# Lightning attention followed by a cosine-gated feed-forward: the loads of q, k and v for two sequences joined into one transfer from the fifth pair on

## The chip, the cores and the metric

The kernel runs on one core of a Trainium2 chip. The metric is the device time of one execution in microseconds. Seven executions of the kernel before gave a median of 203.84 us, from 203.79 to 204.97.

## What is computed

Four sequences of 768 positions, eight heads of 64 channels. The attention is linear with a decay per head: within a block the scores are masked by powers of `lam`, and between blocks a 64 by 64 state per head is carried along. The heads of each position are put together to a row of 512, and a feed-forward layer with the gate h * cos(h) follows.

```python
for b in range(nb):
    intra = einsum('bhic,bhjc->bhij', qb, kb) * Dmask
    intra = einsum('bhij,bhjd->bhid', intra, vb)
    inter = einsum('bhid,bhde->bhie', qb * lam_pow, kv_state)
    out[:, :, sl] = intra + inter
    kv_state = lam_block * kv_state + einsum('bhsd,bhse->bhde', kb * rev_pow, vb)
x = attn_out.transpose(0, 2, 1, 3).reshape(B * S, H * D)      # 3072 x 512
h = x @ w_in                                                   # 3072 x 2048
out = (h * cos(h)) @ w_out                                     # 3072 x 512
```

Inputs and output are float32; the matrix products run in bf16.

## The kernel before

The 3072 positions are cut into 24 blocks of 128. Two blocks make a pair, and there are 12 pairs, counted here from 0 as in the code. Pairs 0 and 1 (`SPANS = 2`) are loaded and computed in a form of their own at the start. From pair 2 on, pair `pr` consists of block `2*pr` and block `2*pr+1`, which are the same 128 positions of two neighbouring sequences (`where`, line 167, gives sequence `b` and position chunk `c`). "The fifth pair" is pair 4, `n = 8` and up.

One pair goes through these steps:

- `add_load` (L289): SyncE starts six transfers, one each of q, k and v for both blocks: `q_f`, `k_f`, `v_f`, tiles of 128 positions by 8 heads by 64 floats, 256 KB each. In HBM 64 floats (256 B) lie together. Each of the three names has six buffers.
- `prepare` (L329): GpSimd turns them into bf16: `prep_q` (L343) scales q, `prep_k` (L347) casts k, both into the halves of one tile `qk`; `prep_v` (L351) scales v into `v_s`. Its order is q, q, k, k, v, v. Pair 2 alone uses VectorE and ScalarE for a part of it.
- From pair 3 on (`DMA_FROM = 6`) SyncE starts two transposing transfers from `qk` into `qkT` (L379), the first for q, the second for k. The first waits for both `prep_q`, the second for both `prep_k`.
- TensorE makes the scores from `qkT` (L421) and the state update from `qk` and `v_s` (L433), VectorE masks the scores (L426) and adds up the state (L439), TensorE makes the values (L484) and adds the part of the carried state (L516), and the result goes to `xT`.
- The feed-forward part takes tiles of two or four blocks (`TILES`): TensorE multiplies `xT` by `w_in` (L746, 16 groups of four matmuls for a tile), ScalarE takes the cosine (L752), VectorE multiplies (L758), TensorE multiplies by `w_out` (L792, 16 matmuls for a block), ScalarE moves the result to `o_sb` (L806), and SyncE stores it (L813, L815).

The order on every engine is fixed when the kernel is built. `Planner.order` (L70) plays all tasks through with the durations that the code gives them, always starting the task that can begin first, and the instructions are written out in the order of the starts. On TensorE a pair's scores are therefore put at the place at which the plan believes its `qkT` to be there. A load is planned as `dma("SP", LOAD_US, 0.85, ...)` (L302): 0.85 us on SyncE's queue, then 1.22 us on the transfer engines, then 1.0 us until it can be read. Each engine carries out its list strictly in order, so an instruction that waits holds up all behind it.

On SyncE's queue the order in the loop is, for one pair: two q loads, two k loads, two v loads, the two transposes, with one or two stores of finished blocks among them. The q load of pair `pr+1` is planned after the second transpose of pair `pr` (L388).

Of the kernel before, what the change touches and what calls it, by code (L numbers as in the profile page):

```python
# [10 lines left out]
F32 = mybir.dt.float32  # L11
# [12 lines left out]
LAG = 2  # L24
ATT = 0.95
LOAD_US = 1.22
ALONE = [3, 4, 5, 6]

APART = [3, 4, 5, 11]
# [113 lines left out]
def kernel(  # L143
# [10 lines left out]
    nc = tc.nc  # L154
    B, H, S, D = q.shape
    P = 128
# [10 lines left out]
    def where(n):  # L167

        if n < 2 * SPANS:
            return n // 2, n % 2  # L170
        g, c = divmod(n // 2, NB)
        return 2 * g + n % 2, c

    BUFS = {"ld": 6, "qk": 3, "v_s": 6, "qkT": 3, "s_m": 4, "cos": 3, "o_sb": 4}
    ctx.enter_context(tc.manual_schedule())
    consts = ctx.enter_context(tc.tile_pool(name="consts", bufs=1))
    loads = ctx.enter_context(tc.tile_pool(name="loads", bufs=BUFS["ld"]))
    toks = ctx.enter_context(tc.tile_pool(name="toks", bufs=4))
    work = ctx.enter_context(tc.tile_pool(name="work", bufs=2))
    psum = ctx.enter_context(tc.tile_pool(name="psum", bufs=1, space=bass.MemoryType.PSUM))  # L180
# [1 line left out]
    def bank(i, shape, dt, name):  # L182
        return psum.tile(shape, dt, tag=f"bank{i}", bufs=1, name=name)
# [54 lines left out]
    w_out_src = moe_w_out.rearrange("(ko ki) m -> ki ko m", ki=P)  # L238
    WCH = 4

    pl = Planner({**BUFS, "q_f": BUFS["ld"], "k_f": BUFS["ld"], "v_f": BUFS["ld"]})
    MM = lambda cols, n=1: n * (cols / 2400.0 + 0.0025)

    SW = 0.11
# [1 line left out]
    live = {}  # L246
# [4 lines left out]
    def prio_attn(n, part):  # L251
        i = next(i for i in range(len(TILES)) if n < first[i + 1])
        return begins[i - 1] + unit[i - 1] * (n - n % 2 - first[i] + 2 * part) / TILES[i]

    load_t, issue_t = {}, {}
    last_issue = {}

    def dma(queue, us, issue_us, emit, prio, deps=(), get=None, ordered=True, lat=1.9):
        t = pl.add(queue, issue_us, list(deps) + [last_issue.get(queue) if ordered else None], emit, prio, get=get)
        if ordered:  # L260
            last_issue[queue] = t
        d = pl.add("DMA", us, [t], None, prio, lat=lat)
        d.issue = t
        return t, d

    def start(queue, o, x, deps):
        i = queue.dma_start(out=o, in_=x)  # L267
        for d in deps:
            tc.add_manual_dep(i.ins, d.issue.ins.ins.name, mybir.DependencyInfo(
                mybir.DependencyClass.Sync, mybir.DependencyReason.DATA), reason="order of loads")  # L270
        return i
# [16 lines left out]

    def add_load(n, name, src, prio, deps=()):  # L289
        b, c = where(n)  # L290

        def emit(_):
            t = loads.tile([P, H, D], F32, tag=name, name=name)
            live[name, n] = t
            i = start(nc.sync, t, src[b, :, c * P:(c + 1) * P, :].transpose([1, 0, 2]), deps)
            if (name, n) == ("q_f", 2 * SPANS):

                tc.add_manual_dep(i.ins, pace[0].ins.ins.name, mybir.DependencyInfo(
                    mybir.DependencyClass.Sync, mybir.DependencyReason.DATA), reason="order of loads")
            return i  # L300

        issue_t[name, n], load_t[name, n] = dma("SP", LOAD_US, 0.85, emit, prio, deps, get=name,  # L302
                                                lat=1.9 if name == "v_f" and n < 2 * SPANS + 2 else 1.0)
        return load_t[name, n]

    w_t, pace = {}, []
# [22 lines left out]
    def prepare(pr):  # L329

        b, c = where(2 * pr)
        early = 2 * pr < TILES[0] + 2
        vec = {"DVE": nc.vector, "POOL": nc.gpsimd}
        us = {"DVE": 0.69, "POOL": 1.05}
        pa = lambda part: prio_attn(2 * pr, part)

        def new_qk():
            if ("qk", pr) not in live:
                live["qk", pr] = toks.tile([P, 2, H, 2, D], BF16, tag="qk", bufs=BUFS["qk"], name="qk")
            return live["qk", pr]  # L340

        def prep_q(_, s, e):
            vec[e].tensor_mul(new_qk()[:, 0, :, s], live.pop(("q_f", 2 * pr + s)),  # L343
                              q_scale[:, c, :].unsqueeze(2).to_broadcast([P, H, D]))

        def prep_k(_, s):
            (nc.scalar.copy if early else nc.gpsimd.tensor_copy)(new_qk()[:, 1, :, s], live.pop(("k_f", 2 * pr + s)))  # L347

        def prep_v(_, s, e):
            live["v_s", 2 * pr + s] = toks.tile([P, H, D], BF16, tag="v_s", bufs=BUFS["v_s"], name="v_s")  # L350
            vec[e].tensor_mul(live["v_s", 2 * pr + s], live.pop(("v_f", 2 * pr + s)),  # L351
                              v_scale[:, c, :].unsqueeze(2).to_broadcast([P, H, D]))

        a, k_ = [], []
        for s in range(2):
            n = 2 * pr + s
            eq = "DVE" if early and s == 0 else "POOL"
            ev = "DVE" if early and s == 1 else "POOL"
            a.append(pl.add(eq, us[eq], [load_t["q_f", n]] + a, partial(prep_q, s=s, e=eq), pa(-0.9), get=None if s else "qk"))
            k_.append(pl.add("ACT" if early else "POOL", 0.61, [load_t["k_f", n]] + ([] if early else [a[0]]), partial(prep_k, s=s), pa(-0.9)))  # L360
            d_t[n] = v_head[n] = pl.add(ev, us[ev], [load_t["v_f", n]], partial(prep_v, s=s, e=ev), pa(-0.85), get="v_s")
            for name, t in (("q_f", a[s]), ("k_f", k_[s]), ("v_f", d_t[n])):
                issue_t[name, n].frees = [t]

        def new_T():
            if ("qkT", pr) not in live:
                live["qkT", pr] = toks.tile([P, 2, H, P], BF16, tag="qkT", bufs=BUFS["qkT"], name="qkT")
            return live["qkT", pr]

        def transposes(t, i):  # L370
            live["t", pr, i] = bank(t.bank[0], [P, H, P], BF16, "ps_t")
            for h in range(H):
                nc.tensor.transpose(live["t", pr, i][:, h, :], live["qk", pr][:, i, h], ident)  # L373

        def transposes_out(_, i):
            nc.vector.tensor_copy(new_T()[:, i], live["t", pr, i])

        def transposes_dma(_, i):
            return nc.sync.dma_start_transpose(out=new_T()[:, i], in_=live["qk", pr][:, i].rearrange("t h s d -> t (h s d)"))  # L379

        for i, src in enumerate((a, k_)):
            get = None if i else "qkT"
            if 2 * pr >= DMA_FROM:
                head, T[pr, i] = dma("SP", 1.4, 1.3, partial(transposes_dma, i=i), 2 * pr + i - LAG + 1.5,
                                     src + ([qkT_head[pr]] if i else []), get=get, ordered=False)
                T[pr, i].lat = 1.2
                if i and 2 * pr + LAG < NBLK:
                    issue_t["q_f", 2 * pr + LAG].deps.append(head)  # L388
            else:
                t = pl.add("PE", MM(P, 8), src + ([T[pr, 0]] if i else []), partial(transposes, i=i), pa(-0.05 + 0.05 * i), banks=1)  # L390
                head = T[pr, i] = pl.add("DVE", 0.7, [t], partial(transposes_out, i=i), pa(0.0), get=get)
                t.bank_frees = [[head]]
            if i == 0:
                qkT_head[pr] = head
        qk_head[pr] = a[0]
# [76 lines left out]
    def add_stretch(pr, ahead=None):  # L472
# [70 lines left out]
        deps = [So[n0], So[n0 + 1], Uo[pr, 0], Uo.get((pr - 1, 1)) if c else None]  # L543
        more = pr + 1 < NBLK // 2 and pr + 1 not in ALONE
        apart = pr in APART
# [279 lines left out]
    names = ORDER.split()  # L825
    for pr in range(SPANS, NBLK // 2):
        for name in "qkv":
            names += [x for x in (f"{name}{2 * pr}", f"{name}{2 * pr + 1}") if x not in names]
    src = {"q": q, "k": k, "v": v}
    kept = []  # L830
    for at, name in enumerate(names):
        which, n = name[0], int(name[1:])
        soft = which in "io"
        deps = [kept[-3 if soft else -2]] if at and (names[at - 1][0] in "io") != soft else []
        if name == f"q{2 * SPANS}":
            deps = []
        if name == f"v{2 * SPANS}":
            deps = [load_t["k_f", 2 * SPANS]]
        if name == "o3":
            deps = [load_t["q_f", 2 * SPANS]]  # L840
# [10 lines left out]
    for pr in range(SPANS, NBLK // 2):  # L851
        prepare(pr)
    first_scores, first_update = add_scores(SPANS, prio_attn(2 * SPANS, 0.2))
    add_span_state(first_scores, prio_attn(2 * SPANS, 0.2))
    pr = SPANS
    for i in range(len(TILES)):
        while 2 * pr < first[i + 1]:
            if pr + 1 in ALONE:
                add_scores(pr + 1, prio_attn(2 * pr + 2, 0.2))
# [64 lines left out]
```

## Time and profile before

The profiled execution took 203.82 us on the device, of which the profile's span covers 202.1 us; 1.7 us lie around it.

| engine | busy us | share of the span | instructions |
|---|---|---|---|
| TensorE, matmuls | 196.9 | 97% | 2469 |
| TensorE, weight loads | 116.8 | 58% | 2469 |
| ScalarE | 120.6 | 60% | 241 |
| VectorE | 116.2 | 57% | 228 |
| GpSimd | 64.8 | 32% | 85 |

| transfers | bytes | share of 16 engines |
|---|---|---|
| started by SyncE and ScalarE (q1) | 28.78 MB | 64.3% |
| started by GpSimd (q0) | 4.72 MB | 16.2% |

Times in the profile count from the start of the span. Busy time is summed by engine; "idle before" is what an engine stood still ahead of an instruction and what ended that; PE is the matmul part of TensorE and PEld its weight loads; SPq is SyncE's queue, where the time of an instruction includes what it is held back by a full queue.

### The profile page before, as it was taken

Reading aid. Unit: us, or ns where it says so; the run is one execution under the profiler, and the core shown is the slowest. Engines: PE = TensorE matmul, PEld = TensorE weight load, DVE = VectorE, ACT = ScalarE, POOL = GpSimd, SP = SyncE. Lnnn points to the kernel's source line nnn. Section 1 sums busy time; section 2 is a strip of 40 time slices with the busy share of each in tenths; the row PEclk is TensorE's granted clock in tenths of the full one; section 3 lists DMA queues with packets and bytes.
Section 4 is the critical chain, followed back from the end, with each engine's and each line's share of the span. In section 5 each row is a group of like instructions: output and inputs, shape, how many; then the busy total and the mean of one; then the engine's idle time right before and its main releaser. Section 6 shows DMA issues by size and latency. Waiting matters only on the chain.

```text
span 202.1 us, 5941 instructions
## 1 busy us (share of the span) xinstructions
PE 196.9 (97%) x2469; PEld 116.8 (58%) x2469; DVE 116.2 (57%) x228; ACT 120.6 (60%) x241; POOL 64.8 (32%) x85
## 2 busy tenths in 40 slices
PE   6999999999999999999999999999999999999994
PEld 2467444557757857767658676755445444444443
DVE  2878773257955958758448575834579544444001
ACT  4978870238838868565639666654877554355120
POOL 5694002076134173645555072533530000000000
PEclk9999999999999999999999999999999999999999
DMA  4999999999989998999999797999950010111112
GB/s 118 324 192 203 203 205 215 175 219 245 212 208 178 241 223 197 248 181 258 202 256 246 175 233 96 269 124 264 243 139 3 3 52 0 52 55 52 52 52 104
DMA packets 96762, 33.94 MB, mean 168 GB/s; under 512 B 84320, under 2 KB 93792, under 8 KB 96736
## 3 DMA queue, kind: packets, MB, share of 16 engines
q1 hardware_dynamic: 89232, 28.78, 64.3%
q0 software_dynamic: 7360, 4.72, 16.2%
q8 instruction: 19, 0.31, 0.7%
q14 instruction: 7, 0.06, 0.1%
q10 hardware_dynamic: 144, 0.07, 0.1%
HBM read 27.27 MB, written 6.29 MB: 166 GB/s over the span
## 4 chain that ended last, share of the span: by engine, by line
PE 93%; DMA 3%; SPq 2%; POOL 1%; issue 0%; ACT 0%; POOLq 0%; ACTq 0%
PE ps_h L746 42%; PE ps_f L792 42%; DMA sp_f<-in_k_dram 3%; PE ps_s L421 2%; PE ps_o L484 2%; PE ps_o L516 2%; PE ps_kv L433 1%; SPq L267 1%; PE ps_o L650 1%; PE ps_kv L637 1%; POOL k_sp L605 1%; PE ps_x L484 0%; PE ps_t L373 0%; PE ps_t L613 0%; PE ps_s L624 0%; PE ps_o L656 0%
## 5 line engine op out<-in xcount | busy, mean ns | idle before, releaser
L758 DVE TENSOR_TENSOR g<-ps_h,cos 128x256 bf16<-128x256 f32 (+1 forms) x148 | 73.2, 503 | 43.1 <-ACT cos L752 42.1
L752 ACT ACTIVATE cos<-ps_h,halfpi 128x256 f32<-128x256 f32 (+1 forms) x148 | 75.7, 539 | 29.4 <-PE ps_h L746 28.6
L792 PE MATMUL ps_f<-w_out_sb,g 128*128 128x512 bf16 (+2 forms) x400 | 91.5, 371 | 0.0
L746 PE MATMUL ps_h<-xT,w_in_sb 128*128 128x256 bf16 (+1 forms) x592 | 91.3, 304 | 0.0
L746 PEld LDWEIGHTS <-w_in_sb 128*128 128x128 bf16 x592 | 57.1, 98 | 30.1 <-DVE xT L524 0.4
L792 PEld LDWEIGHTS <-g 128*128 128x128 bf16 x400 | 37.7, 98 | 37.3
L343 POOL TENSOR_TENSOR qk<-q_f,q_scale 128x512 bf16<-128x512 f32 x19 | 19.8, 1056 | 35.1 <-DMA q_f<-in_q_dram 31.9
L806 ACT COPY o_sb<-ps_f 128x512 f32<-128x512 f32 (+1 forms) x24 | 13.8, 573 | 24.7 <-PE ps_f L792 24.7
L351 POOL TENSOR_TENSOR v_s<-v_f,v_scale 128x512 bf16<-128x512 f32 x19 | 19.7, 1043 | 17.8 <-DMA v_f<-in_v_dram 12.7
L426 DVE TENSOR_TENSOR s_m<-ps_s,mask 128x512 bf16<-128x512 f32 x20 | 13.0, 685 | 4.2 <-PE ps_s L421 3.6
L347 POOL CAST qk<-k_f 128x512 bf16<-128x512 f32 x18 | 11.0, 614 | 10.4 <-DMA k_f<-in_k_dram 10.3
L524 ACT CAST xT<-ps_o 128x512 bf16<-128x512 f32 x11 | 6.0, 588 | 9.2 <-PE ps_o L516 5.8
L439 DVE TENSOR_TENSOR sum<-sum,ps_kv 128x512 f32<-128x512 f32 x15 | 10.2, 681 | 0.6
L444 ACT CAST S<-sum 128x512 bf16<-128x512 f32 x15 | 9.2, 617 | 0.9 <-DVE sum L439 0.8
L267 POOL DMA_DIRECT2D w_out_sb<-in_moe_w_out_dram x4 | 3.0, 776 | 15.9 <-DMA q_f<-in_q_dram 15.9
L806 DVE COPY o_sb<-ps_f 128x384 f32<-128x384 f32 x1 | 0.6, 558 | 11.6 <-PE ps_f L792 11.6
L884 PE MATMUL ps_idle<-blank 128*128 128x512 f32 (+2 forms) x8 | 5.4, 824 | 1.6 <-DVE blank L210 1.6
L484 PEld LDWEIGHTS <-v_s 64*64 64x64 bf16 x320 | 3.9, 107 | 4.4 <-issue 3.0
L629 DVE TENSOR_TENSOR s_m_sp<-ps_s,mask_sp 128x512 bf16<-128x512 f32 x8 | 5.0, 682 | 1.0 <-PE ps_s L624 1.0
L501 DVE COPY spare<-ps_o 1x1 f32<-1x1 f32 x6 | 0.9, 156 | 8.0 <-PE ps_o L484 8.0
L484 PE MATMUL ps_o<-s_m,v_s 64*64 64x64 bf16 x256 | 5.1, 196 | 0.0
L535 DVE TENSOR_TENSOR xT<-ps_o,cross 128x256 bf16<-128x256 f32 x8 | 3.1, 422 | 3.0 <-PE ps_o L516 2.9
(74 smaller groups left out, 92.9 us busy)
## 6 DMA issues: line engine op xcount, KB each, us to landing
q_f<-in_q_dram SPq DMA_DIRECT2D x20, 256.0 KB, 4.1
k_f<-in_k_dram SPq DMA_DIRECT2D x20, 256.0 KB, 4.6
v_f<-in_v_dram SPq DMA_DIRECT2D x20, 256.0 KB, 5.2
out_dram<-o_sb SPq DMA_DIRECT2D x19, 256.0 KB, 2.6
w_out_sb<-in_moe_w_out_dram POOLq DMA_DIRECT2D x4, 512.0 KB, 12.5
sp_f<-in_q_dram SPq DMA_DIRECT2D x2, 512.0 KB, 5.3
sp_f<-in_k_dram SPq DMA_DIRECT2D x2, 512.0 KB, 5.7
w_in_sb<-in_moe_w_in_dram POOLq DMA_DIRECT2D x4, 256.0 KB, 6.8
```

The source lines that it names most:

```text
L343: vec[e].tensor_mul(new_qk()[:, 0, :, s], live.pop(("q_f", 2 * pr + s)), q_scale[:, c, :].unsqueeze(2).to_broadcast([P, H, D]))
L347: (nc.scalar.copy if early else nc.gpsimd.tensor_copy)(new_qk()[:, 1, :, s], live.pop(("k_f", 2 * pr + s)))
L351: vec[e].tensor_mul(live["v_s", 2 * pr + s], live.pop(("v_f", 2 * pr + s)), v_scale[:, c, :].unsqueeze(2).to_broadcast([P, H, D]))
L426: nc.vector.tensor_mul(t, live["s", pr][s], mask.unsqueeze(1).to_broadcast([P, H, D]))
L439: nc.vector.tensor_add(new, live["sum", pr, 0] if half else live["sum", pr - 1, 1], live["kv", pr][half])
L444: nc.scalar.copy(new_S(pr, half), live["sum", pr, half])
L484: yield lambda h=h: nc.tensor.matmul(o[halves[h % 2], h // 2], lhsT=live["v_s", n0 + s][m, h, :], rhs=live["s_m", n0 + s][m, h, :], start= ...
L746: nc.tensor.matmul(t[:, :n], lhsT=w_in_sb[:, kd, f * P:(f + 1) * P], rhs=live["xT", i][:, kd, at], start=(kd == 0), stop=(kd == KD - 1))
L752: nc.scalar.activation(c[:, :n], live["h", i, f, at.start][:, :n], AF.Sin, bias=halfpi)
L758: return nc.vector.tensor_mul(live["g", i][:, f, at], live.pop(("h", i, f, at.start))[:, :n], live.pop(("c", i, f, at.start))[:, :n])
L792: nc.tensor.matmul(live["f", i, j, piece][:, :width], lhsT=live["g", i][:, f, j * P:(j + 1) * P], rhs=w_out_sb[:, f, part], start=(f == 0) ...
L806: (nc.scalar.copy if eng == "ACT" else nc.vector.tensor_copy)(o[:, :width], live["f", i, j, piece][:, :width])
```

## The change

From pair 4 on one transfer carries both blocks of a pair, for q, for k and for v: 24 transfers of 512 KB take the place of 48 of 256 KB. The tiles `q_f`, `k_f`, `v_f` now hold both blocks, with three buffers of twice the size in place of six, for all pairs; pairs 2 and 3 fill the two halves by a transfer each as before. The six `prepare` operations of a pair stay as they are, but from pair 4 on both blocks' operations wait for the same transfer. In the plan the joined load stands with 1.2 us on SyncE's queue and 2.1 us on the transfer engines.

```diff
+PAIRED = 4
-    loads = ctx.enter_context(tc.tile_pool(name="loads", bufs=BUFS["ld"]))
+    loads = ctx.enter_context(tc.tile_pool(name="loads", bufs=BUFS["ld"] // 2))
-    pl = Planner({**BUFS, "q_f": BUFS["ld"], "k_f": BUFS["ld"], "v_f": BUFS["ld"]})
+    pl = Planner({**BUFS, **{name: BUFS["ld"] // 2 for name in ("q_f", "k_f", "v_f")}})
     def add_load(n, name, src, prio, deps=()):
         b, c = where(n)
+        both = n >= 2 * PAIRED
         def emit(_):
-            t = loads.tile([P, H, D], F32, tag=name, name=name)
-            live[name, n] = t
-            i = start(nc.sync, t, src[b, :, c * P:(c + 1) * P, :].transpose([1, 0, 2]), deps)
+            if n % 2 == 0:
+                t = loads.tile([P, 2, H, D], F32, tag=name, name=name)
+                live[name, n], live[name, n + 1] = t[:, 0], t[:, 1]
+            if both:
+                i = start(nc.sync, t.rearrange("u b h d -> u (b h) d"),
+                          src[b:b + 2, :, c * P:(c + 1) * P, :].rearrange("b h u d -> u (b h) d"), deps)
+            else:
+                i = start(nc.sync, live[name, n], src[b, :, c * P:(c + 1) * P, :].transpose([1, 0, 2]), deps)
...
-        issue_t[name, n], load_t[name, n] = dma("SP", LOAD_US, 0.85, emit, prio, deps, get=name,
+        issue, load_t[name, n] = dma("SP", 2.1 if both else LOAD_US, 1.2 if both else 0.85, emit, prio, deps, get=None if n % 2 else name,
                                                 lat=1.9 if name == "v_f" and n < 2 * SPANS + 2 else 1.0)
+        if n % 2 == 0:
+            issue_t[name, n] = issue
+            issue.frees = []
+            issue_t[name, n + 1] = issue_t[name, n]
+            if both:
+                load_t[name, n + 1] = load_t[name, n]
...
-                issue_t[name, n].frees = [t]
+                issue_t[name, n].frees.append(t)
...
-            names += [x for x in (f"{name}{2 * pr}", f"{name}{2 * pr + 1}") if x not in names]
+            names += [x for x in (f"{name}{2 * pr}", f"{name}{2 * pr + 1}") if x not in names and (pr < PAIRED or x == f"{name}{2 * pr}")]
```

## The prediction

> **What bounds the kernel now.** I read the chain that ended last first, then the busy table by stretches, then SyncE's queue and the landings of the transposes.
>
> The page's parts 1 to 4:
>
> ```profile
> PE 196.9 (97%) x2469; PEld 116.8 (58%) x2469; DVE 116.2 (57%) x228; ACT 120.6 (60%) x241; POOL 64.8 (32%) x85
> PEclk9999999999999999999999999999999999999999
> DMA  4999999999989998999999797999950010111112
> q1 hardware_dynamic: 89232, 28.78, 64.3%
> q8 instruction: 19, 0.31, 0.7%
> PE 93%; DMA 3%; SPq 2%; POOL 1%; issue 0%; ACT 0%; POOLq 0%; ACTq 0%
> ```
>
> The busy table of the loop, and three pieces of the chain in order of time (start, us, what):
>
> ```profile
> 66.00:149.00 83.00, 83.00 (x1285) 54.66 (x1284) 54.30 (x117) 55.59 (x120) 37.81 (x43) 1.00 1.05 219
> ...
> 127.76 0.26 PE ps_s L421 x32
> ...
> 138.72 0.30 PE ps_s L421 x32
> ...
> 152.23 0.26 PE ps_s L421 x32
> ```
>
> TensorE is busy for 83.00 of 83.00 us at full clock: after its start at 11.4 us it never waits until 199.2. But the transfer engines are as full (share 1.05) up to slice 29, about 150 us. Two resources run level; the kernel ends with TensorE only because every pair's `qkT` comes just in time. SyncE's queue around the last two pairs, and the transposes of pair 10 in a window of their own:
>
> ```profile
> 128.22 3.84 SPq L267 DMA_DIRECT2D v_f<-in_v_dram  x2
> 132.17 4.22 SPq L379 DMA_TRANSPOSE qkT<-qk  x2
> 136.48 0.53 SPq L815 DMA_DIRECT2D out_dram<-o_sb  x1
> 137.07 1.19 SPq L267 DMA_DIRECT2D q_f<-in_q_dram  x2
> ```
>
> ```profile
> L379 SPq DMA_TRANSPOSE qkT<-qk x2: 1737/2060/2384, 132.2 to 134.0; - x2
> DMA to landing us min/median/max: 4.5/5.1/5.6
> ```
>
> The second transpose starts at 134.0 and lands 4.5 us later, at 138.5; pair 10's scores begin at 138.72. Done so for pairs 4 to 11, the landings are 68.1, 78.1, 90.6, 101.4, 112.1, 126.1, 138.5 and 149.6, and the scores start at 69.24, 80.82, 91.93, 104.22, 116.34, 127.76, 138.72 and 152.23. The slack is 0.2 to 4.2 us. Pairs land 11.6 us apart ((149.6 - 68.1) / 7).
>
> **A gain is hardly possible.** The matmuls of the changed kernel are the same ones, in another order, the order up to pair 3's attention is untouched, and so is the end. There is no TensorE wait to remove. I exclude a gain but for 0.1 to 0.3 us of chance.
>
> **Step 1: what moves on TensorE.** The plan believes in 2.1 us for a joined load where it had 2 x 1.22, and pulls the scores forward. Counting matmuls ahead of each pair's scores in the two orders, the changed kernel has fewer there: pair 4, 8 of 128x256; pair 5, 12 and 4 of 128x512; pair 6, 8 and 4; pair 7, 8 and 12; pair 8, 24 and 12; pair 9, 20 and 12; pair 10, 12 and 28; pair 11, 44 of 128x512. The chain prices eight 128x256 at 0.87 us (0.109 each) and eight 128x512 at 1.73 (0.216 each). So the scores are due earlier by 0.87, 2.18, 1.74, 3.47, 5.22, 4.78, 7.37 and 9.52 us, that is at 68.4, 78.6, 90.2, 100.8, 111.1, 123.0, 131.4 and 142.7, if TensorE is never held up. With the old landings pair 10 would be 138.5 + 0.2 - 131.4 = 7.3 us late and pair 11 149.6 + 0.2 - 142.7 = 7.1 (0.2 us is what lay between landing and scores at pair 10). TensorE's list is strict: behind waiting scores stand the values of the pair before, the feed-forward matmuls, and all that ScalarE and VectorE make of them. The delays don't add up: a pair late by 5 us has made room for the next, so the end moves by the largest lateness. All hangs on how much the landings gain. To gain nothing and lose nothing, the cycle would have to shrink from 11.6 to 10.6 us ((142.7 - 68.4) / 7).
>
> **Step 2: what the joined load saves in transfer time.** No run shows it. Far row: the four `sp_f` loads, 512 KB each in runs of 512 B, land from 5.5 (1.3 + 4.3) to 10.1, 1.53 us apart. Near row: two `q_f` at 77.2 and 77.6 land after 4.5 and 5.0, 0.9 us apart, so 1.8 for 512 KB in runs of 256 B. The joined load keeps 256 B runs. Bounds per pair: from 0 to 3 x (1.8 - 1.53) = 0.8 us. I take 0.25, nearer the near row; over the six cycles to pair 10 that is 1.5 us.
>
> The Trainium skill, "DMA: Bandwidth & Descriptors", section "Rules for kernel authors", would have small transfers coalesced into one large one, as each bears a fixed cost of about 2.0 us by its section "Anatomy of one DMA". By that an estimate would save up to 6 us for a pair, if the loads came one after another; the landings 0.9 us apart show that they overlap. By the rule the time would stay at 203.8, by the rows it does not.
>
> **Step 3: what it saves on SyncE's queue.** Three issues for a pair go. An unhindered issue takes 0.37 us, and they are not the limit: the two `v_f` above took 3.84 us and the two transposes 4.22 because the queue was full or the copies late. I book nothing. The cover is that backlog; without it, 3 x 0.4 = 1.2 us for a pair would be gained, more than the 1.0 needed.
>
> **Step 4: what is lost by waiting for both halves.**
>
> SyncE's own waits (us in total, times, longest):
>
> ```profile
> SPq L379 <- POOL v_s L351: 10.3, 9, 2.6
> SPq L379 <- POOL qk L347: 10.2, 7, 2.5
> ```
>
> Of 18 transposes 16 stood still for GpSimd, 20.5 us in all (some put down to v_s, though they wait for the q and k copies ahead of it). Before, the first block's cast (0.61 us, L347) ran while the second block's load was still coming; now both follow the joined landing, so the second transpose can start 0.61 us later, and the next q load behind it too. At pair 10 the second cast ran from 133.21 to 133.83 and the transpose began at 134.01, right behind it; at others the queue was blocked longer than that. Bounds: 0, and 0.61 x 6 = 3.7 us up to pair 10. I take one such delay, 0.6 us. GpSimd itself is covered: its six operations take 2 x 1.05 + 2 x 0.61 + 2 x 1.04 = 5.4 us of each 11.6. The last `prep_v` ends 1.04 us later against the v landing than before; the update (L433) needs it, but only after the transposes.
>
> In the same page's section "Why a DMA increments its semaphore by 16 and not by 1" the skill says that only the full count means that all data has landed, and that a count in between doesn't tell which bytes have. By it nothing of the first half can be used early, so the delay of step 4 would stand in every pair, and the sum would be the second rival's below; no run here shows a transfer used before its end.
>
> **Step 5: queue order.** In the changed list a pair's q load comes ahead of a store instead of behind it, and one store fewer stands ahead of pair 10's transposes (those of blocks 0 to 11 instead of 0 to 12), two fewer at pair 11. A 256 KB store among loads takes about 0.7 us: a k load landed at 105.1, the store behind it at 105.8. I book -0.7 for pair 10 and -1.4 for pair 11. At pair 4 the k and v loads are issued some 2 us earlier, but behind a full pipe; bounds 0 and -2, I take -0.5, as the work ahead is the same.
>
> **The sum.** Pair 10 lands at 138.5 - 1.5 + 0.6 - 0.7 - 0.5 = 136.4, and its scores could begin at 136.6 instead of 131.4: 5.2 us late. Pair 11: 149.6 - 1.75 + 0.6 - 1.4 - 0.5 = 146.6, 4.1 late, covered by the 5.2. The profiled execution, 202.1 us of span and 1.7 around it, becomes 203.82 + 5.2 = 209.0; the median of 203.84 says the same.
>
> **The rivals.** *The bytes flow as in the far row* (not slower): place, the transfer engines; price, 0.8 us for a pair, with the -0.5 and the stores 0.8 x 6 + 0.5 + 0.7 = 6.0 of the 7.3 at pair 10, and a part of the queue's 1.2 of step 3 closes the rest. It decides from 1.0 us for a pair on ((7.3 - 0.5 - 0.7) / 6). For it: the plan's 2.1 us is 0.34 below two single loads. Against: the runs stay 256 B. Then 203.8.
>
> *GpSimd becomes the bound of the cycle*: all six delays of 0.61 and no byte saved: 138.5 + 3.7 - 0.7 - 0.5 + 0.2 - 131.4 = 9.8 late, 213.6. For it: 16 waits of the transposes for GpSimd. Against: its 5.4 us of 11.6, and that in most cycles the queue's backlog was longer.
>
> *Instruction loads fall otherwise*: the 19 packets of q8 each hold one of the 16 transfer engines, and the transposes wait for the last engine. In the cycles of 14.0 and 12.4 us before pairs 9 and 10 they come twice. If they miss the loads, two cycles shrink by 1.5 us: 2.2 late, 206.0. This is within my range.
>
> **How the numbers follow.** 0.3% (0.6 us) is about what a measurement can tell from no change. Forecast, 2 to 8.5 us late: 0.73, likeliest 209.0. Far-row bytes: 0.12, same. GpSimd's bound: 0.10. A real gain: 0.02; the rest, a slip of 0.6 to 2 us, 0.03. Slower 0.73 + 0.10 + 0.03 = 0.86, same 0.12, faster 0.02. The range reaches from 0.4 us above no change to 0.8 short of the second rival and leaves out most of both, 0.2 together: 204.2 to 212.8.
>
> **What would show it.** Right: gaps on PE ahead of L421, named as waits for the qkT transfer, none before pair 6, most at pairs 9 and 10; PE busy still 196.9 in a longer span; landings of the transposes 11 to 11.7 us apart. Step 2 is wrong if the joined loads follow each other by 1.6 us or less; step 4 if the second transpose starts well after the second cast everywhere; all of it if the landings come 10.6 apart. No PE gap at all would make the prediction wrong.

## The result and the profile after

The changed kernel takes 206.0 us (median of 13 runs, 204.01 to 209.07); the kernel before, run beside it, 203.86 (33 runs, 203.72 to 204.97). The ratio is 1.0077, with a 95% interval from 1.0056 to 1.0098. The ratios here and below leave out executions that took over 1.5% more than the shortest of the same kernel (here three above 208 us), while medians and ranges count all. The changed kernel is slower, as forecast, but by some 2 us and not by 5.2. In two further lots it took 204.9 and 204.45; over all 35 runs the mean is 205.5, and twelve of them are below 204.5. The kernel before spreads far less.

The profiled execution of the changed kernel took 206.19 us, with a span of 204.5. Parts 1 to 6 of its page, the lines that answer to those of before, and the groups of the scores (line 421 has become 435, line 379 393):

```profile
PE 197.4 (97%) x2469; PEld 116.9 (57%) x2469; DVE 115.5 (56%) x228; ACT 120.3 (59%) x241; POOL 64.5 (32%) x85
...
PEclk9999999999999999999999999999999999999999
DMA  4999999988799999999899999999310110111112
...
q1 hardware_dynamic: 88848, 28.78, 60.8%
...
q8 instruction: 19, 0.31, 0.6%
...
PE 71%; DMA 20%; SPq 4%; POOL 2%; ACT 1%; issue 1%; POOLq 0%; ACTq 0%
...
L435 PE MATMUL ps_s<-qkT 64*64 64x64 bf16 x320 | 4.4, 195 | 1.8 <-DMA qkT<-qk 1.7
...
q_f<-in_q_dram SPq DMA_DIRECT2D x8, 512.0 KB, 4.5
k_f<-in_k_dram SPq DMA_DIRECT2D x8, 512.0 KB, 6.2
v_f<-in_v_dram SPq DMA_DIRECT2D x8, 512.0 KB, 7.1
```

The work is the same 2469 matmuls at full clock, but the chain that ended last now runs through transfers for 20% of the span instead of 3%, and the scores stand still for `qkT`. The span grew by 2.4 us (202.1 to 204.5): 0.5 us more busy time of TensorE and 1.9 us of standing still. The busy table by stretches (columns as before: length, PE, PEld, DVE, ACT, POOL, clock, transfer share, GB/s):

```profile
66.00:133.00 67.00, 65.73 (x1090) 45.53 (x1087) 44.90 (x103) 45.23 (x102) 33.38 (x38) 1.00 1.03 224
133.00:148.00 15.00, 14.44 (x285) 8.19 (x286) 10.04 (x18) 9.45 (x17) 5.48 (x7) 1.00 0.85 178
...
66.00:149.00 83.00, 81.17 (x1380) 54.20 (x1378) 55.18 (x121) 55.41 (x121) 38.86 (x44) 1.00 0.99 214
```

TensorE was busy for 83.00 of these 83.00 us before; now 81.17. By 149 us it has more matmuls on record, 1380 against 1285: the small matmuls of the scores and of what hangs on them come earlier. The chain of the changed kernel, in order of time (start, us, what), shows where it stands still; two pieces of it:

```profile
68.99 6.02 DMA k_f<-in_k_dram
75.07 1.18 POOL qk L361 x2
76.26 2.77 DMA qkT<-qk
...
123.08 6.26 DMA k_f<-in_k_dram
129.40 1.18 POOL qk L361 x2
130.60 1.23 SPq L393
...
134.51 6.68 DMA v_f<-in_v_dram
141.20 3.83 DMA qkT<-qk
```

At pair 5 and at pair 10 the chain runs through a joined k load, GpSimd's two casts and a transpose, at pair 11 through a joined v load and the transpose behind it in the queue. The second transposes of pairs 4 to 11 land at 68.6, 79.0, 91.1, 101.8, 112.0, 123.0, 133.3 and 145.0, 10.9 us apart; the scores start at 68.65, 79.08, 91.12, 101.81, 112.17, 124.02, 133.39 and 145.07. Against the due times of step 1 they are 0.2, 0.5, 0.9, 1.0, 1.1, 1.0, 2.0 and 2.4 us late. Pairs 8 and 9 did not wait themselves (0.2 and 1.0 us lie between landing and scores); they carry the lateness of pair 7. The last figure is the 2.4 us of the span.

### The profile page after: what moved, and what is told of

Read it like the earlier page. It is cut to its first block, busy times and chain, and to the rows that moved or that the text cites. A ratio compares the mean times of both kernels' runs of the same rounds, so it can differ in the third digit from the quotient of the medians.

```text
span 204.5 us, 5924 instructions
## 1 busy us (share of the span) xinstructions
PE 197.4 (97%) x2469; PEld 116.9 (57%) x2469; DVE 115.5 (56%) x228; ACT 120.3 (59%) x241; POOL 64.5 (32%) x85
## 4 chain that ended last, share of the span: by engine, by line
PE 71%; DMA 20%; SPq 4%; POOL 2%; ACT 1%; issue 1%; POOLq 0%; ACTq 0%
PE ps_f L806 32%; PE ps_h L760 31%; DMA k_f<-in_k_dram 9%; DMA qkT<-qk 5%; DMA v_f<-in_v_dram 3%; DMA sp_f<-in_k_dram 3%; SPq L269 2%; POOL qk L361 1%; PE ps_s L435 1%; PE ps_o L530 1%; SPq L829 1%; PE ps_kv L447 1%; PE ps_o L498 1%; ACT cos L766 1%; SPq L393 1%
## 5 line engine op out<-in xcount | busy, mean ns | idle before, releaser
L760 PE MATMUL ps_h<-xT,w_in_sb 128*128 128x256 bf16 (+1 forms) x592 | 93.6, 304 | 0.0
L806 PE MATMUL ps_f<-w_out_sb,g 128*128 128x512 bf16 (+2 forms) x400 | 93.3, 371 | 0.0
L361 POOL CAST qk<-k_f 128x512 bf16<-128x512 f32 x18 | 10.6, 614 | 11.4 <-DMA k_f<-in_k_dram 11.4
L435 PE MATMUL ps_s<-qkT 64*64 64x64 bf16 x320 | 4.4, 195 | 1.8 <-DMA qkT<-qk 1.7
L435 PEld LDWEIGHTS <-qkT 64*64 64x64 bf16 x320 | 3.4, 108 | 3.5 <-DMA qkT<-qk 3.0
```

Of the source, the lines that this page charges most:

```text
L435: nc.tensor.matmul(live["s", pr][s][m, h, :], lhsT=kT[r, h, m], rhs=qT[r, h, m], start=True, stop=True, skip_group_check=True)
L760: nc.tensor.matmul(t[:, :n], lhsT=w_in_sb[:, kd, f * P:(f + 1) * P], rhs=live["xT", i][:, kd, at], start=(kd == 0), stop=(kd == KD - 1))
L806: nc.tensor.matmul(live["f", i, j, piece][:, :width], lhsT=live["g", i][:, f, j * P:(j + 1) * P], rhs=w_out_sb[:, f, part], start=(f == 0) ...
```

## The experiments

Each kernel was timed beside the kernel before; of the kernel before itself two further profiles were taken, of one execution each. "Single" is a load of 256 KB for each block, "joined" one of 512 KB for both. The kernel before took 203.85, 203.87 and 203.83 us in the three lots.

**The changed kernel again** (no edit), to see how far its executions differ.

> The changed kernel once more, on the chip of the next three. Both theories: about 206 us, single executions between 204 and 209, as the lateness of pairs 9 to 11 differs from one execution to the next.

Measured: 204.9 us (204.0 to 206.54, 11 runs), ratio 1.0062 (1.0034 to 1.009). The profiled execution was a short one, 204.05 us: `qkT` landed at 67.2, 77.0, 89.0, 99.2, 109.2, 121.0, 130.9 and 142.3, and no scores waited; at the last two pairs 0.4 and 0.5 us were left. Between this execution and the first profile the same landings differ by 1.4 to 2.8 us, and TensorE has no such reserve left.

**The old order with joined loads.** The kernel before on all engines, but from pair 4 on the first of two loads brings both blocks and the second brings nothing.

```diff
+            if n >= 2 * PAIRED:
+                if n % 2:
+                    return None
+                return start(nc.sync, t.rearrange("u b h d -> u (b h) d"),
+                             src[b:b + 2, :, c * P:(c + 1) * P, :].rearrange("b h u d -> u (b h) d"), deps)
...
```

> The plan of before (TensorE, ScalarE, VectorE and GpSimd in exactly the old order), but from pair 4 on each pair's loads go out as one joined transfer at the place of the first of the two. Theory O (the loss comes from the scores being pulled forward, the joined load itself costs nothing): 203.8 to 204.0 us, no wait of L421 for qkT over 0.3 us. Rival G (waiting for both halves on GpSimd delays the transposes by 0.6 us in a pair): landings late by up to 0.6 us a pair, so waits before the scores of pairs 9 and 10, whose slack was 1.6 and 0.2 us: 204.5 to 207.

Measured: 203.93 us (203.79 to 205.42, 12 runs), ratio 1.0006 (0.9987 to 1.0025). Joining in the old order makes no difference that can be told from none. The loss is in the order. The profiled execution was the longest of the twelve, 205.42, and in it scores did wait (line 421 is 428 here; us in total, times, longest):

```profile
PE ps_s L428 <- DMA qkT<-qk: 1.4, 2, 0.7
```

So "no wait over 0.3 us" was a miss for that execution. The two waits stood ahead of pairs 4 and 6, not of 9 and 10 as rival G had it, and single executions of the kernel before reach 205.4 too.

**The changed order with single loads.** All four engines and SyncE's queue as in the changed kernel, but two transfers in each place.

```diff
-                i = start(nc.sync, t.rearrange("u b h d -> u (b h) d"),
-                          src[b:b + 2, :, c * P:(c + 1) * P, :].rearrange("b h u d -> u (b h) d"), deps)
+                for x in range(2):
+                    i = start(nc.sync, t[:, x], src[b + x, :, c * P:(c + 1) * P, :].transpose([1, 0, 2]), deps)
```

> The plan of the changed kernel (all four engines in exactly its order), but each pair's loads go out as two transfers of 256 KB at the place of the joined one. Theory O with the old landings carried over: pair 10 7.3 us late less about 1.2 for the queue order, so 209 to 211 us, some 4 us more than the changed kernel: joining then brings the landings forward by 0.6 us for a pair. Rival P (the landings are set by the place of stores and loads in the queue, not by joining): 205.5 to 206.5 us, the same as the changed kernel. Rival G: faster than the changed kernel, 204 to 205, as the first cast can start on the first half.

Measured: 204.41 us (203.79 to 207.06, 12 runs), ratio 1.002 (1.0006 to 1.0033). The 209 to 211 of my own theory were a miss: without any gain from joining, the new order still lands pair 10 at 132.9 and pair 11 at 144.9. The transfers had come earlier for another reason. The median lies in the range of rival G, 0.5 us below that of the joined kernel in the same lot (204.9); whether joining costs these 0.5 us is tried again below.

**Only k single**, q and v joined, in the changed order, to take the wait for both halves away from the second transpose.

```diff
-            if both:
+            if both and name == "k_f":
+                for x in range(2):
+                    i = start(nc.sync, t[:, x], src[b + x, :, c * P:(c + 1) * P, :].transpose([1, 0, 2]), deps)
+            elif both:
```

> The changed kernel with its plan, q and v joined, k as two transfers. In the changed profile the second transpose starts 1.25 to 1.6 us after the k landing in every pair. If that is the bound (G), the first cast comes 0.6 us earlier and so does every cycle: pairs 9 to 11 lose up to 4 us of lateness, 203.9 to 204.5 us. If the transfers themselves are the bound (O), the second transpose waits for the v load anyway: 205.5 to 206.5.

Measured: 205.53 us (203.94 to 206.56, 7 runs), ratio 1.007 (1.0043 to 1.0098), landings of pairs 10 and 11 at 133.7 and 145.4. No gain: the delay of step 4 is there in the changed kernel, but taking it away from k brought nothing that can be seen.

**The kernel before, twice more**, one execution each, to see whether the landings carried into the prediction come again.

> The kernel before, for a second profile: second transposes of pairs 9, 10 and 11 landed at 126.1, 138.5 and 149.6 us in the first. Theory Q (the queue's order sets the landings): again within 1.5 us of these. Rival R (the first profile of before was a late one, and a lateness must not be carried over from one execution): pair 10 at 134 to 136.5, pair 11 at 145 to 148.

> The kernel before, once more, for a third set of landings. If the landings carried into the prediction (126.1, 138.5, 149.6 for pairs 9, 10 and 11) were typical, they come again within 1 us. If they were those of one late execution, pair 9 lands at 122 to 124 and pair 10 at 133 to 136, as in the second look; and if the store of block 13 sets when pair 11's q load starts, pair 11 lands at 147 to 150 in every look, since TensorE's clockwork sets that store.

Measured: 203.77 and 203.82 us. Pair 10 landed at 134.0 and 137.5 (138.5 in the first profile), pair 11 at 147.8 and 147.9 (149.6). So the first profile was the latest of three, but pair 10 came late in the third too: "one late execution" is only a part of it. Pair 11 keeps the bound that was expected of it; pair 9's landing is missing from both traces. SyncE's queue in the timeline of the third profile (start, us, what):

```profile
129.16 4.48 SPq L379 DMA_TRANSPOSE qkT<-qk  x2
134.31 0.36 SPq L815 DMA_DIRECT2D out_dram<-o_sb  x1
134.71 1.35 SPq L267 DMA_DIRECT2D q_f<-in_q_dram  x1
```

The second line is the store of block 13; ScalarE's copy that fills it, from the timeline of the same execution:

```profile
133.70 0.58 ACT L806 COPY o_sb<-ps_f 128x512 f32<-128x512 f32 x1
```

The transposes of pair 10 were through at 133.64 (129.16 + 4.48), but the store of block 13 stood at the head of the queue until the copy ended at 134.28, and behind it the q load of pair 11. In the second profile the queue stood from 131.91 to 134.26:

```profile
127.17 4.74 SPq L379 DMA_TRANSPOSE qkT<-qk  x2
134.26 0.36 SPq L815 DMA_DIRECT2D out_dram<-o_sb  x1
```

In these two executions TensorE's own output held the queue back, for 0.6 and 2.3 us, so pair 11's landing near 148 wasn't set by the transfers alone. SyncE's queue in the changed kernel, from its timeline:

```profile
128.00 3.83 SPq L393 DMA_TRANSPOSE qkT<-qk  x2
131.92 0.53 SPq L829 DMA_DIRECT2D out_dram<-o_sb  x1
132.50 0.42 SPq L269 DMA_DIRECT2D q_f<-in_q_dram  x1
132.98 1.49 SPq L269 DMA_DIRECT2D k_f<-in_k_dram  x1
134.51 3.38 SPq L269 DMA_DIRECT2D v_f<-in_v_dram  x1
137.99 1.70 SPq L829 DMA_DIRECT2D out_dram<-o_sb  x1
```

Here the store behind the transposes is that of block 12, whose copy ended at 127.3, and the store of block 13 (copy ended at 136.6) comes behind the v load. The q load of pair 11 starts at 132.5 instead of 134.7, and in other executions at 129.6 and 129.9.

**Only the queue's order changed.** Single loads and the old order on TensorE, ScalarE, VectorE and GpSimd; SyncE's list alone is taken from a plan that is told shorter loads. It comes near the changed kernel's list but isn't the same: the same stores stand ahead of pair 10's transposes, but the store of block 13 stands between the two transposes of pair 11 instead of ahead of both, and some other stores are one place off.

```diff
+    SINGLE, FAST = (LOAD_US, 0.85), (1.05, 0.6)
+    queue = [t for t in planned(*FAST) if t.eng == "SP" and t.emit]
+    rest = [t for t in planned(*SINGLE) if t.eng not in ("SP", "DMA")]
...
```

> Single loads; TensorE, ScalarE, VectorE and GpSimd in the old order, SyncE's queue in the order that comes out when the plan is told 1.05 us for a load instead of 1.22 (q ahead of stores, one or two stores fewer ahead of the last transposes). Theory Q: landings of pairs 10 and 11 near those of the new plan with single loads, 132.9 and 144.9, 4 to 5 us earlier than in the kernel before, and no wait on TensorE: 203.8 to 203.9. Rival N (the engines' new order brings the landings forward): landings as before, 138.5 and 149.6. Rival R: no difference to the second profile of before.

Measured: 203.99 us (203.8 to 204.57, 10 runs), ratio 1.0003 (0.9988 to 1.0018). Pair 10 lands at 133.6 and pair 11 at 145.6: against the mean of the three profiles of the kernel before (136.7 and 148.4) 3.1 and 2.8 us earlier. Against the second of them, taken on the same chip in the same lot, it is 0.4 and 2.2 us: at pair 10 that is no difference that one execution can show, as rival R had it, at pair 11 the landing lies 2.2 us below the earliest of the three. The time doesn't show it, since the old scores aren't due before 138.7 and 152.

**Joined loads planned as long as two single ones**: the changed kernel, but the plan believes 2.44 us, and 1.7 on the queue.

```diff
-        issue, load_t[name, n] = dma("SP", 2.1 if both else LOAD_US, 1.2 if both else 0.85, emit, prio, deps, get=None if n % 2 else name,
+        issue, load_t[name, n] = dma("SP", 2.44 if both else LOAD_US, 1.7 if both else 0.85, emit, prio, deps, get=None if n % 2 else name,
```

> The changed kernel with one number changed: the plan is told 2.44 us and 1.7 us of queue for a joined load, what it was told for two single ones. The scores then stand within 1 us of their old places (pair 10 due at 138.7, pair 11 at 152.2). If the loss comes from the places of the scores and not from the transfers: 203.8 to 204.0, no wait of L435 over 0.3 us. If joined transfers are slow in themselves: above 204.5.

Measured: 203.88 us (203.84 to 204.16, 12 runs), ratio 0.9997 (0.9984 to 1.0009); 1.5 to 4.4 us are left at every pair, and no scores wait. The only waits ahead of the scores that this trace shows are not for a transfer (us in total, times, longest):

```profile
PEld L435 <- issue: 1.3, 4, 0.4
```

With the same transfers and other numbers in the plan, from which the order on the engines and in SyncE's queue follows, the loss is gone.

**Joined loads planned shorter still**, 1.8 us, to pull the scores further ahead.

```diff
-        issue, load_t[name, n] = dma("SP", 2.1 if both else LOAD_US, 1.2 if both else 0.85, emit, prio, deps, get=None if n % 2 else name,
+        issue, load_t[name, n] = dma("SP", 1.8 if both else LOAD_US, 1.2 if both else 0.85, emit, prio, deps, get=None if n % 2 else name,
```

> The changed kernel with the plan told 1.8 us for a joined load, what 512 KB take by the landings. The scores are then due at 67.5, 77.3, 90.2, 96.0, 111.1, 123.0, 131.4 and 141.9 us. With the landings of the two profiles of the changed kernel (68.6 and 67.2, 79.0 and 77.0, 101.8 and 99.2 for pair 7, 145.0 and 142.3 for pair 11) pair 7 is late by 3.2 to 5.8 and the rest follows: 207 to 210 us, slower than the changed kernel. If the landings follow the plan, as joined loads that are really faster would: 205 to 206.

Measured: 208.58 us (205.25 to 209.92, 6 runs), ratio 1.0123 (1.0073 to 1.0172). The waits of the scores, from the view of waits of this kernel (us in total, times, longest):

```profile
PEld L435 <- DMA qkT<-qk: 4.9, 3, 3.3
...
PE ps_s L435 <- DMA qkT<-qk: 4.3, 2, 3.2
```

The scores of pair 7, which this order has due at 96.0, start at 100.43 as `qkT` lands at 100.39: 4.4 us late, as expected. The ratio rests on the three shortest of the six executions (205.25, 206.39, 207.89); the trace is that of the longest. Told 2.44, 2.1 and 1.8 us, the plan gives medians of 203.9, 204.5 to 206.0 and 208.6: the loss follows the number in the plan.

**Joined beside single once more**, both in the changed order and in one lot, since the first lot had them at 204.9 and 204.41.

> The changed kernel, unaltered, beside the kernel with the same order on all engines but two transfers of 256 KB for each of q, k and v (next run), on one chip and against the same runs of the kernel before. Theory A (the loss comes from the scores that the plan pulls forward, and joining adds or saves nothing of its own): 205 to 206, and the two kernels agree within 0.3%. Theory B (joining costs in addition, because both blocks' casts wait for the joined landing: 0.61 us later start of the second transpose): the single-transfer kernel is 0.6 to 1.3 us faster, as it looked across two different lots of runs (204.4 against 205.9).

> The changed kernel's order on all four engines and on SyncE's queue, with two transfers of 256 KB in the place of each joined one. Theory A: 205 to 206, like the changed kernel beside it within 0.3%. Theory B: 204.2 to 204.8, at least 0.6 us below the changed kernel.

Measured: joined 204.45 us (203.8 to 206.3, 11 runs), ratio 1.0052 (1.0018 to 1.0086); single 204.63 (203.8 to 206.09, 12 runs), ratio 1.004 (1.0017 to 1.0064). They agree within 0.1%, so theory A holds in this, though both medians are below its 205 to 206. The executions of both spread over 2.5 us. Over both lots the means are 205.1 (22 executions, joined) and 204.9 (24, single): a cost of joining of some tenths of a us isn't shown and isn't excluded.

No kernel of these was faster than the kernel before.

## Why the prediction was half right

**What bounds the kernel: right.** No run went below 203.7 us; the order that left 2.2 to 6.9 us between landing and scores (the queue's order alone) gained nothing.

**Step 1, the scores pulled forward: right, to 0.3 us.** Where nothing held TensorE up, in the profile of the changed kernel run beside the single loads, the scores of pairs 4 to 11 started at 68.24, 78.52, 90.06, 100.53, 110.90, 122.75, 131.14 and 142.58, against 68.4, 78.6, 90.2, 100.8, 111.1, 123.0, 131.4 and 142.7 counted from the matmuls. It is also the cause of the loss: with 2.44 in the plan it is gone, and with single loads in the same order it is there. That the delays don't add up was right as well: the span grew by the 2.4 us of the latest pair.

**The sum failed, in its landings: "Pair 10 lands at 138.5 - 1.5 + 0.6 - 0.7 - 0.5 = 136.4".** It landed at 133.3 in the profiled execution and at 131.6 in the mean of three. The mechanism, scores placed ahead of their data, was right; what failed is the size of two terms, the start and what the new order does to the landings (step 5). Term by term, with the means of the profiles:

| term | pair 10, booked | measured | pair 11, booked | measured |
|---|---|---|---|---|
| start (before) | 138.5 | 136.7 | 149.6 | 148.4 |
| step 2, bytes | -1.5 | 0.0 | -1.75 | -0.1 |
| step 4, both halves | +0.6 | in the line above | +0.6 | in the line above |
| step 5, the queue's order (a list near the new one) | -0.7 - 0.5 | -3.1 | -1.4 - 0.5 | -2.8 |
| the rest of the new order, on the four engines and in the queue | none | -2.0 | none | -2.4 |
| landing | 136.4 | 131.6 | 146.6 | 143.1 |

The measured columns are worked out thus: the three profiles of the kernel before; from there to the kernel with only the queue's order changed (one profile); from there to the two profiles of the changed order with single loads (132.9 and 130.2; 144.9 and 141.5); from there to the three of the changed kernel (133.3, 130.9, 130.6; 145.0, 142.3, 142.1).

The term that was most mis-sized is what the new order does to the landings: step 5 booked 1.2 us at pair 10 and 1.9 at pair 11, and the two rows of the order come to 5.1 and 5.2. Their sum is firm in its sign: all six profiles of the new order, with joined loads, single ones or k alone single, land pair 10 at 130.2 to 133.7 and pair 11 at 141.5 to 145.4, all three of the old at 134.0 to 138.5 and 147.8 to 149.6. How it divides between the two rows isn't shown: one profile stands between them, executions of one kernel differ by 2 to 4.5 us there, and against the profile from its own chip that run gains 0.4 and 2.2 us, at pair 11 about what step 5 booked.

One mechanism is seen. I priced the stores that move by the 0.7 us that their bytes cost, but a store also costs what it waits for: that of block 13 held the queue until TensorE had finished that block. In the first profile the wait couldn't be seen, as the transposes ended at 136.39, after the copy (134.28). The second error is the start: I took landings from one execution where three give 134.0 to 138.5. At pair 10 the order makes the forecast landing 3.9 us too late and the start 1.8; steps 2 and 4, booked at -0.9 together and measured at none, take 0.9 off again, which leaves the 4.8 us between 136.4 and 131.6. Where the rest of the order's gain comes from stays open.

So the latest pair is 11 and not 10, and its lateness is 143.1 + 0.05 - 142.7 = 0.5 us by the mean of the three profiles, 2.4 in the first of them, and 1.5 by the mean of all runs (205.5 - 204.0), where 5.2 were booked. Two of the three profiled executions were short ones (204.05 and 203.93), so the measured columns stand for executions that land somewhat early.

**Step 2: the near row was right, and the 0.25 us for a pair still too generous.** In the first profile of the changed kernel the joined v follows the joined k by 1.67 to 1.89 us where they run one behind the other (129.35 to 131.02, 75.01 to 76.90), twice the 0.9 us of single ones. No saving is to be seen. The rule of the Trainium skill weighed there ("DMA: Bandwidth & Descriptors", section "Rules for kernel authors"), that small transfers are to be coalesced, finds no gain in these runs: old order with joined loads, ratio 1.0006. The 2.0 us weighed beside it are given there for transfers issued by GpSimd; these are issued by SyncE.

**Step 3: right, nothing.** Fewer issues brought nothing in the old order.

**Step 4: the delay is there, the price isn't.** GpSimd's two casts follow each joined k landing, and from pair 5 on the second transpose begins within 0.4 us of their end (129.40 + 1.18, transpose at 130.60). But k in two transfers gave 205.53, and all in two 204.63 against 204.45: no gain to be seen. What the transposes land after is, it seems, what stands ahead of them in the queue: in the profile of the changed kernel the first transpose of pairs 4 to 11 lands 0.9 to 1.4 us after the last load or store ahead of it (pair 11: store 143.29, transpose 144.19). By the skill's statement on the full count ("DMA: Bandwidth & Descriptors", section "Why a DMA increments its semaphore by 16 and not by 1") the delay would stand in every pair, which these runs agree with, and cost 213.6 by the second rival, which they don't.

**The rivals.** *The bytes flow as in the far row*: no; yet what it said of the end, that the landings keep up with the scores, came true in a third of the executions (12 of 35 within 0.7 us of the kernel before), with no byte saved: single loads in the same order land as early. *GpSimd becomes the bound*: no, as the k loads in two show. *Instruction loads fall otherwise*: its time, 206.0, is the one measured, but that is luck. The long cycles that it named, 14.0 us ahead of pair 9 and 12.4 ahead of pair 10, shrink in the three profiles of the changed kernel to 11.0 to 11.8 and 9.7 to 10.3 (111.98 to 123.03, 123.03 to 133.34 in the first). But in all three the packets of q8 still come twice in pair 9's cycle, and once instead of twice in pair 10's; and in the second profile of the kernel before the two cycles took 22.4 us together (111.53 to 133.95) instead of 26.4, with all four packets in them. The packets alone don't set the length; what one of them costs was not tried.

**The marks.** Gaps on PE ahead of L435, named for `qkT`: seen. PE busy still 196.9: 197.4. Landings 10.9 apart lie between the 11 to 11.7 of the forecast and the 10.6 that would have made all of it wrong, and 10.7 in the two other profiles. Gaps "none before pair 6, most at 9 and 10" was wrong: they are small and spread over pairs 4 to 7, 10 and 11.

## What to carry to other kernels

Before carrying the landing times of a profile over to another order, ask what set each of them: here a load behind a store waited for the engine that fills the store. In this kernel, where two resources run level, the duration that the plan was told for a transfer decided the time, not the way the transfer was cut: a number too small pulls the consumer ahead of its data. Take such times from several executions: those of one kernel differed here by up to 4.5 us at one pair.

## What the hardware showed unexpectedly

**After a long wait the clock was lower too.** With 1.8 us in the plan TensorE stood still for 3.2 us ahead of pair 7. The busy table around it (length, PE, PEld, DVE, ACT, POOL, clock, transfer share, GB/s):

```profile
97.00:100.40 3.40, 0.24 (x16) 0.12 (x16) 0.16 (x1) 0.47 (x1) 2.04 (x2) 1.00 1.08 177
100.40:103.00 2.60, 2.23 (x98) 1.80 (x100) 1.88 (x4) 1.03 (x2) 0.00 (x0) 0.50 1.13 258
103.00:105.00 2.00, 2.00 (x15) 1.42 (x14) 0.46 (x2) 0.69 (x3) 1.83 (x2) 0.80 1.17 313
105.00:107.00 2.00, 2.00 (x16) 1.32 (x14) 1.67 (x5) 1.68 (x5) 0.22 (x1) 1.00 1.01 232
```

After the wait the granted clock was 0.50 until 103 and full again by 105, an estimated loss of 1.7 us (2.6 x 0.5 + 2.0 x 0.2): pair 7's scores were 4.4 us late, pair 8's, which waited for nothing, 5.8 (116.94 against 111.1). That is one trace, of the longest execution; all three executions above 209 us have a mean clock of 0.992, the three shorter ones 0.998 to 1.000. The waits of the changed kernel, 0.9 us at most, were followed by no such fall: the clock stands at 1.00 in its stretches above. The Trainium skill, "TensorE: Matmul & The Clock Gate", section "Part 1: The HAM clock gate (the "warmup" mystery)", has the clock fall to half after an idle window of about 3.4 us; the wait of 3.2 us here is a little shorter than that.

**Executions of one kernel differ, and by more where no reserve is left.** The changed kernel spreads from 203.8 to 209.1 us, the kernel before from 203.7 to 205.5, the joined loads planned as two from 203.84 to 204.16. In the trace of the first profile of the changed kernel the landings were already 1.4 to 2.3 us later at pairs 3 and 4 than in the other two (55.3 and 68.6, against 53.0 to 53.1 and 66.9 to 67.2), and at pair 11 still 2.7 to 2.9. What starts such a delay isn't known.
